# Attention in front of two mixture layers: memory product as two column halves, deeper buffers, a new table of task priorities

## The chip, the cores and the metric

The kernel runs on one core of a Trainium2 chip, in one launch. The metric is the device time of that launch in microseconds (us), the median of several runs; less is better.

## What is computed

Three stages in float32 (B, H, S, D = 4, 8, 576, 64; 2304 tokens, width 512):

```python
scores = where(causal, -1e9, scale * q @ k.T)          # per batch and head
local  = softmax(scores) @ v
q_p    = where(q > 0, q, exp(q) - 1) + 1                # the features
mem    = (q_p @ M_prev) / (q_p @ z_prev + 1e-6)
x      = g * mem + (1 - g) * local                      # g = sigmoid(beta), one per head
x      = (silu(x @ w_gate) * (x @ w_val)) @ w_out       # first layer, d_ff 1536
out    = quadratic_gate(x @ w_in) @ w_out2              # second layer, d_ff 2048
```

## The kernel before, in words

**Two plans.** The program is recorded as tasks. A task has an engine, an estimated duration, a priority number, the tasks that it needs and the buffer places that it holds. `Plan.order` (line 179 on) walks through an estimated time and on each engine starts the ready task of the lowest number, provided that free places are there; the order so found is emitted, and each engine then runs its own list strictly in that order. There are two plans. The first holds the attention and the part of the first layer that can be done early; the second holds the rest of the two layers. The second plan's lists are the same in both kernels.

**The first plan.** The attention is cut into 16 pairs (4 batches x 4 pairs of heads), `Attention.pair`, line 400 on. For a pair:

- SP loads K, Q, V, z and M (`load`, `load_v`, `load_z`, `load_M`).
- PE transposes K and Q into `K`, `S` (`tk`, `tm`, `tq`, lines 497 to 509).
- Features: ACT `min` and `exp`, VectorE (DVE) `phi`, then GpSimd (POOL) `w` and two `fold` (lines 540 to 551, tile `e`), DVE `nrm`, POOL `pn` (line 561, tile `p`); PE transposes `p` (`tp`, lines 567 and 570) into `P`.
- Scores: PE multiplies query chunk c (0 to 3) with the c+1 key chunks that the mask leaves, both heads side by side in the row halves of the array (`qk`, line 611; tiles `s0c` and `s1c` for the two heads), and the last 64 queries of both heads in one full product (`qk4`, line 642, tiles `s40`, `s41`). DVE adds the mask and takes the minimum (`mx`, line 622), ACT takes the exponential and its sum (`ex`, line 629) into the probability tiles `a0` to `a3`, and `a4`.
- DVE adds up and inverts the sums of a head, POOL scales each probability tile (`.sc`, line 697, nine per pair), PE transposes it (`t4`, `t03`, `t02`, `t01`, `t13`, `t12`, `t11`; lines 708, 710, 731, 748), ACT or DVE copies it to the tiles `R0`, `R1` (`.cp`, line 436; the table `COPY` names the engine).
- Output: `av1` (256 columns) and `av0` (320 columns) add the memory product (line 775, one product on the whole array: `MZ` is block diagonal over the two heads) and the products of V with the transposed probabilities, the two heads side by side in the column halves of the array (line 782). ACT and DVE split the result into `x`, and SP stores it to `xs` in DRAM (`x_out`, line 805).

The same plan decodes 12 weight units of the first layer: ACT and DVE steps, then three POOL instructions (lines 875, 878, 911). `EARLY` holds the priorities of the 12. As soon as 512 tokens of `xs` are there, `load_x` fetches them as four tiles `xh` (there are four places, so a group of tokens waits for the one before), and `early_unit` multiplies them (line 1031; 12 matmuls per unit, in two tasks of six, 36 units in all). ACT copies the result to `gvo`, and it is stored. These 432 matmuls depend on nothing of the pair at work, so they are PE's filler. `GROUP_AT` and `X_AT` are their priorities.

**What sets the order.** A task's number is 100 times the number of its pair plus the entry of its name in the table `ORDER`. The entries before reach from about -2300 to 2700, so the name counts for as much as several pairs.

**Places.** `AB` is the number of places for each of the tiles `a0` to `a3`, of which a pair needs two. `RB1` and `RB0` are the places per head for `R1` and `R0`. The tiles `e`, `p` and `x` have one place each (`plan.cap`, line 340 on).

Of the kernel before, what the change touches and what calls it, by code (L numbers as in the profile page):

```python
# [10 lines left out]
F32R = mybir.dt.float32r  # L11
# [7 lines left out]
P = 128  # L19
B, H, S, D = 4, 8, 576, 64  # L20
# [8 lines left out]
D1 = 8  # L29
UNITS1 = 12  # L30
BANKS = 5
AB, RB1, RB0 = 2, 1, 1
NOACT = 4
AHEAD = 30
CUTS = (0, 2, 4)
EARLY = (-695.6332, 2783.9892, 1285.5157, 4826.1976, -587.204, 1099.0329, 1783.7958, 812.7126, 3810.6396, 6743.5654, -296.1106, 490.4918)
XH, GVO = 4, 3
OWN = 2
XB, OP, RAW, HP, TP, WA = 12, 5, 3, 3, 3, 5
# [1 line left out]
UNITS, HALVES = 20, 5  # L41
PHASES = (2, 3, 3)

GROUP_AT, X_AT = (38662.3623, 35325.2542, 46229.556), (412.8002, 381.1663, 182.3662)

FIRST = (0, 8, 1, 2, 9, 3, 4, 10, 5, 6, 11, 7)
BLOCK = 512
# [13 lines left out]


ORDER = {
    "load": -940.6324,
    "load_v": 203.5903,
    "load_z": -887.0432,
    "load_M": -747.8821,
    "tk": -333.4689,
    "tm": -812.4048,
    "tq": 461.8326,  # L70
    "tk.cp": -890.2619,
    "tm.cp": 1721.9097,
    "tq.cp": 1307.1915,
    "min": 1423.9267,
    "exp": 311.185,
    "phi": 204.0583,
    "w": -1122.4349,
    "fold": -293.9033,
    "nrm": -731.8656,
    "pn": 1733.8628,  # L80
    "tp": 580.7614,
    "tp.cp": -62.0868,
    "tp4.cp": -2.2349,
    "qk": -1311.8398,
    "mx0": -1620.4126,
    "ex0": -960.1039,
    "mx1": -339.7968,
    "ex1": 2676.0763,
    "qk4": 521.5218,
    "mx4": -2277.3531,  # L90
    "ex4": 135.8776,
    "sum0": -780.2454,
    "sum1": -1647.8821,
    "t4.sc": 1505.0802,
    "t4": 592.7662,
    "t4.cp": 1106.002,
    "t03.sc": 264.3754,
    "t03": -818.1143,
    "t03.cp": -181.4909,
    "t02.sc": 771.2966,  # L100
    "t02": 487.7659,
    "t02.cp": -616.6291,
    "t01.sc": 772.9989,
    "t01": -20.2777,
    "t01.cp": -716.0608,
    "t13.sc": 304.2471,
    "t13": -447.9362,
    "t13.cp": -1725.7614,
    "t12.sc": 567.7268,
    "t12": -326.082,  # L110
    "t12.cp": 134.7649,
    "t11.sc": -27.9381,
    "t11": 430.1817,
    "t11.cp": -973.0528,
    "av0": 39.9166,
    "av0.hi": -241.9974,
    "av0.lo": 159.5083,
    "av1": -394.4432,
    "av1.hi": -361.6833,
    "av1.lo": -1110.4372,  # L120
    "x_out": 105.4227,
}
COPY = {"tk": "ACT", "tm": "ACT", "tq": "DVE", "tp": "ACT", "tp4": "ACT", "t4": "ACT", "t03": "ACT", "t02": "ACT", "t01": "DVE", "t13": "ACT", "t12": "DVE", "t11": "DVE"}


def f32(ap):
# [3 lines left out]
class Inst:  # L130


    def __init__(self, tag):
        self.tag, self.left, self.held, self.slot = tag, 0, False, None


class Plan:
# [4 lines left out]
    LAT = {"PE": 220, "ACT": 165, "DVE": 150, "POOL": 120, "SP": 650, "DMA": 950}  # L142
    RELEASE = 90

    def __init__(self, start=None, over=0):

        self.over = over
        self.tasks, self.caps, self.taken, self.start = [], {}, {}, start or {}
# [10 lines left out]
    def add(self, eng, dur, prio, fn, deps=(), uses=(), lat=0, behind=None, port=False):  # L159


        t = {"eng": eng, "port": port, "dur": dur + (0 if eng in ("SP", "DMA") else self.over), "prio": (prio, len(self.tasks)), "fn": fn, "uses": list(dict.fromkeys(uses)),
             "lat": lat + self.LAT[eng], "next": [], "follow": [], "wait": 0, "n": len(self.tasks)}
        for d in deps:
            d["next"].append(t)
            t["wait"] += 1
        for x in ([] if behind is None else behind if isinstance(behind, list) else [behind]):
            x["follow"].append(t)
            t["wait"] += 1
        for u in t["uses"]:  # L170
            u.left += 1
        self.tasks.append(t)
        return t
# [99 lines left out]
def c_fp(*cols):  # L273
    return sum(4 * n / 2.4 + 5 for n in cols) + 30


def c_two(*cols):


    return sum(4 * n / 2.4 + 5 for n in cols) + 2 * max(cols) / 2.4 + 30  # L280


def c_tr(n):
# [40 lines left out]
class Attention:  # L324
# [3 lines left out]
    def __init__(self, ctx, tc, plan, q, k, v, M_prev, z_prev, beta, cst, xs):  # L328
        self.tc, self.nc, self.plan = tc, tc.nc, plan
        nc = tc.nc  # L330
# [1 line left out]
        self.ident = cst["ident"]  # L332
        self.xs = xs
        pool = lambda name, bufs: ctx.enter_context(tc.tile_pool(name=name, bufs=bufs))
        self.ld, self.bt, self.ph = pool("ld", 2), pool("bt", 2), pool("ph", 1)
        self.st, self.ap, self.at = pool("st", 2), pool("ap", AB), pool("at", 1)
        self.sm, self.ac = pool("sm", 3), pool("ac", 1)
        self.ps = ctx.enter_context(tc.tile_pool(name="aps", bufs=1, space=PSUM))
        for tags, n in ((("kn", "qn", "vn", "zb", "a4", "K", "S", "P", "QZ", "MZ"), 2),
                        (("a0", "a1", "a2", "a3"), AB), (("R1_0", "R1_1"), RB1),  # L340
                        (("R0_0", "R0_1"), RB0), (("e", "p", "x"), 1), (("mn",), 3), (("bank",), BANKS)):
            for t in tags:
                plan.cap(t, n)

# [55 lines left out]
    def pair(self, b, n):  # L400
# [6 lines left out]
        nc, pl = self.nc, self.plan  # L407
# [7 lines left out]
        def add(eng, dur, name, fn, deps=(), uses=(), port=False):  # L415
            t = pl.add(eng, dur, num * 100 + ORDER[name], fn, deps, uses, port=port)
            t["name"] = name
            return t
# [179 lines left out]
        def scores(c):  # L598
# [6 lines left out]

            def qk():
                out = [psum(f"s{h}{c}", places[h]) for h in range(2)]
                step = kl // 2 if kl > 256 else kl
                for k0 in range(0, kl, step):
                    for h in range(2):  # L610
                        nc.tensor.matmul(out[h][:, k0:k0 + step], st["S"][halves[h], c * P:(c + 1) * P],  # L611
                                         st["K"][halves[h], k0:k0 + step], start=True, stop=True,
                                         tile_position=(h * 64, 0), skip_group_check=True)

            t_q = add("PE", c_two(kl), "qk", qk, [t_k, t_S], [*places, i_K, i_S, i_a[0, c], i_a[1, c]])
            for h in range(2):
# [138 lines left out]

        def mk_x():
            if "x" not in st:
                st["x"] = self.at.tile([P, 2, S], F32R, name="x", tag="x")
            return st["x"]

        def av(rg, deps):
# [10 lines left out]

            def f():
                o = psum(name, i_o)
                nc.tensor.matmul(o[:, 0:w], MZ().rearrange("p h d -> p (h d)"), st["P"][:, q0:q0 + w],  # L775
                                 start=True, stop=False, skip_group_check=True)
                for i, (c0, c1, kc, at_) in enumerate(terms):
                    n_ = c1 - c0
                    for h in range(2):
                        R = mk_R(rg, h)  # L780
                        r = R[:, at_:at_ + n_] if rg else R[:, at_[0], at_[1]:at_[1] + n_]
                        nc.tensor.matmul(o[halves[h], c0:c1], st["vn"][:, kc, h], r, start=False,  # L782
                                         stop=i == len(terms) - 1, tile_position=(0, h * 64), skip_group_check=True)
# [4 lines left out]
            def lo():  # L788
                nc.vector.tensor_sub(mk_x()[:, 1, q0:q0 + w], st[name][:, 0:w], f32(mk_x()[:, 0, q0:q0 + w]))

            cols = [c1 - c0 for c0, c1, *_ in terms]
            t = add("PE", c_fp(w) + c_two(*cols), name, f, deps + t_P + [l_v, t_M],
                    [i_o, i_P, i_v, i_M, *(i_R1, i_R0)[rg]])
            t = add("ACT", c_act(w), name + ".hi", hi, [t], [i_o, i_x])
            return add("DVE", c_dve2(w), name + ".lo", lo, [t], [i_o, i_x])
# [240 lines left out]
def tile_attention_two_moe(  # L1036
# [76 lines left out]


    with ExitStack() as actx:
        plan = Plan(over=50)
        wts.pooled = True
        wts.begin(actx, plan, {"raw": 2, "wA": 3, "wS": 1}, "a", "pool")
        plan.cap("w1", UNITS1)
# [463 lines left out]
```

## Time and profile before

| | |
|---|---|
| median of 3 runs | 1101.46 us (1099.88 to 1101.58) |
| profiled execution, own time | 1103.3 us |
| its span, first to last instruction | 1101.5 us |
| mean granted TensorE clock | 0.985 of full speed |
| PE busy over the span | 1058.4 us (96%) |
| POOL busy over the span | 212.9 us (19%), all of it in the first plan |

The profile shows one execution. A busy share over the whole span is an average of stages with different limits, so the stretch of the first plan has to be looked at by itself: its last attention product starts at 303.86 us, and its last filler ends where the second plan's matmuls run on without a break, at 363.80 us.

### The profile page before, as it was taken

What the parts mean: (1) busy time and instruction counts of PE and PEld (TensorE: products, weight loads), DVE (VectorE), ACT (ScalarE), POOL (GpSimd) and SP (SyncE); (2) the same over time, 40 slices, a digit from 0 to 9 for tenths busy, and PEclk for the clock granted to TensorE, in tenths of its full rate; (3) what the DMA queues carried; (4) which work ended last, traced back from release to release, by engine and by line L of the source; (5) the groups of instructions that cost most, each with busy time, mean ns of one, the idle gap of its engine ahead of it and who ended that gap; (6) DMA issues with size and microseconds to landing.
All of it is one profiled execution on the core that took longest, in us unless ns stands there. A gap on an engine that the chain in (4) does not pass through costs nothing.

```text
span 1101.5 us, 17845 instructions
## 1 busy us (share of the span) xinstructions
PE 1058.4 (96%) x6160; PEld 883.5 (80%) x6160; DVE 666.0 (60%) x1514; ACT 579.6 (53%) x1330; POOL 212.9 (19%) x285
## 2 busy tenths in 40 slices
PE   5779999999989999999999999999999999999998
PEld 3546677777778988888988888888899999899997
DVE  5767755655400687886867866673656668543443
ACT  6668777777511244543544434464555555444443
POOL 5888976654500000000000000000000000000000
PEclk9689999999999999999999999999999999999999
DMA  5464644444282888983995869999898887955422
GB/s 138 126 180 129 182 119 114 129 124 143 88 272 90 278 309 300 331 292 98 370 339 187 317 246 346 371 361 412 341 376 295 328 317 286 405 192 194 173 77 77
DMA packets 175722, 260.19 MB, mean 236 GB/s; under 512 B 71952, under 2 KB 100624, under 8 KB 175632
## 3 DMA queue, kind: packets, MB, share of 16 engines
q1 hardware_dynamic: 175056, 258.00, 67.3%
q8 instruction: 49, 0.80, 0.3%
q10 hardware_dynamic: 576, 1.05, 0.2%
q14 instruction: 41, 0.34, 0.1%
HBM read 177.21 MB, written 81.79 MB: 235 GB/s over the span
## 4 chain that ended last, share of the span: by engine, by line
PE 77%; DMA 2%; POOL 1%; DVE 1%; ACT 1%; issue 1%; DVEq 0%; ACTq 0%; POOLq 0%
PE mm L1031 25%; PE acc L1523 18%; PE mm L1272 16%; PE acc L1367 13%; PE av L782 2%; PE s L611 1%; POOL a L697 1%; DMA xs<-x 1%; PE av L775 1%; PE t L731 1%; DMA xh<-xs 1%; PE t L748 0%; PE s L642 0%; ACT t L1256 0%; ACT a L629 0%
## 5 line engine op out<-in xcount | busy, mean ns | idle before, releaser
L1523 PE MATMUL acc<-wu,h 128*128 128x512 f32 x864 | 211.1, 392 | 5.0 <-DVE h L1189 4.0
L1031 PE MATMUL mm<-xb,wu 128*128 128x512 f32 (+1 forms) x1008 | 202.4, 360 | 0.0
L1031 PEld LDWEIGHTS mm<-xb,wu 128*128 128x128 f32 x1008 | 171.1, 190 | 28.4
L1523 PEld LDWEIGHTS acc<-wu,h 128*128 128x128 f32 x864 | 157.4, 189 | 35.1 <-DVE h L1189 2.3
L1272 PE MATMUL mm<-xb,wu 128*128 128x256 f32 x1296 | 168.4, 283 | 0.6 <-ACT mm L1343 0.6
L1272 PEld LDWEIGHTS mm<-xb,wu 128*128 128x128 f32 x1296 | 164.1, 192 | 4.8 <-ACT mm L1343 1.0
L1367 PE MATMUL acc<-h,wu 128*128 128x512 f32 (+1 forms) x720 | 151.7, 368 | 0.0
L1367 PEld LDWEIGHTS acc<-h,wu 128*128 128x128 f32 x720 | 125.6, 189 | 22.3
L1186 ACT CAST h<-t 128x512 fp32r<-128x512 f32 (+1 forms) x140 | 80.5, 577 | 80.4 <-DVE t L1262 31.2
L1256 ACT ACTIVATE t<-mm,half 128x512 f32<-128x512 f32 (+1 forms) x80 | 51.6, 645 | 120.8 <-PE mm L1272 74.0
L1031 PE MATMUL mm<-xh,wu 128*128 128x512 f32 x432 | 111.6, 407 | 2.8 <-DMA xh<-xs 2.8
L1189 DVE TENSOR_TENSOR h<-t,h 128x512 fp32r<-128x512 f32 (+1 forms) x140 | 88.1, 635 | 41.4 <-ACT h L1186 40.6
L697 POOL TENSOR_SCALAR a<-a,r,OGP 128x512 f32<-128x512 f32 (+3 forms) x144 | 97.4, 686 | 30.0 <-PE tk L497 14.3
L1031 PEld LDWEIGHTS mm<-xh,wu 128*128 128x128 f32 x432 | 79.7, 190 | 20.4 <-issue 3.6
L1262 DVE SCALAR_TENSOR_TENSOR t<-mm,t 128x512 f32<-128x512 f32 (+1 forms) x80 | 50.9, 636 | 73.9 <-ACT t L1259 73.9
L1079 ACT COPY gvo<-mm 128x512 f32<-128x512 f32 (+1 forms) x80 | 42.7, 542 | 79.6 <-PE mm L1031 74.7
L629 ACT ACTIVATE a<-a,mn 128x512 f32<-128x512 f32 (+3 forms) x128 | 70.9, 556 | 18.4 <-DVE mn L622 17.7
L622 DVE CUSTOM_DVE_ANT_0 a<-s,mask 128x512 f32<-128x512 f32 (+3 forms) x128 | 56.9, 485 | 21.1 <-PE s L611 18.1
L848 ACT ACTIVATE wA<-raw 128x512 f32<-128x512 f32 x64 | 42.6, 670 | 45.7 <-DMA raw<-in_moe_w_in_dram 15.2
L611 PE MATMUL s<-K,S 64*128 64x256 f32 (+2 forms) x384 | 52.0, 392 | 2.3 <-DVE mn L622 2.3
L782 PEld LDWEIGHTS av<-R,vn 128*64 128x64 f32 x448 | 30.2, 139 | 28.5 <-issue 10.3
L782 PE MATMUL av<-R,vn 128*64 128x320 f32 (+4 forms) x448 | 52.0, 371 | 0.1
(123 smaller groups left out, 1375.2 us busy)
## 6 DMA issues: line engine op xcount, KB each, us to landing
xb<-ys SPq DMA_DIRECT2D x93, 512.0 KB, 7.5
park<-wu SPq DMA_DIRECT2D x40, 512.0 KB, 7.4
wu<-park SPq DMA_DIRECT2D x40, 512.0 KB, 9.0
xb<-xs SPq DMA_DIRECT2D x32, 512.0 KB, 7.5
gv<-gv SPq DMA_DIRECT2D x32, 512.0 KB, 7.3
ys<-yo SPq DMA_DIRECT2D x31, 512.0 KB, 6.7
gv<-gvo SPq DMA_DIRECT2D x60, 256.0 KB, 2.3
raw<-in_moe_w_out_dram SPq DMA_DIRECT2D x28, 512.0 KB, 6.4
```

Of the source, the lines that this page charges most:

```text
L611: nc.tensor.matmul(out[h][:, k0:k0 + step], st["S"][halves[h], c * P:(c + 1) * P], st["K"][halves[h], k0:k0 + step], start=True, stop=True ...
L622: nc.vector.tensor_tensor_reduce(a, st[f"s{h}{c}"][:, 0:kl], self.mask0[:, 512 - kl:512], -0.125, 3.0e38, ALU.add, ALU.min, mn[:, o:o + 1])
L629: nc.scalar.activation(a, a, AF.Exp, bias=mn[:, o:o + 1], scale=-1.0, accum_out=sm[:, o, 0:1])
L697: nc.gpsimd.tensor_scalar(a, a, st["mn"]["r"][:, o:o + 1], self.OGP[:, n, o:o + 1], op0=ALU.mult, op1=ALU.mult)
L782: nc.tensor.matmul(o[halves[h], c0:c1], st["vn"][:, kc, h], r, start=False, stop=i == len(terms) - 1, tile_position=(0, h * 64), skip_grou ...
L1031: nc.tensor.matmul(out, kt_of(unit, pw, kt), x[kt][:, px, cols], start=(kt == 0 and i == 0), stop=(kt == KT - 1 and i == 2))
L1186: nc.scalar.copy(s["h"][:, 0], s["t"])
L1189: nc.vector.tensor_sub(s["h"][:, 1], s["t"], f32(s["h"][:, 0]))
L1256: nc.scalar.activation(mk_t(o), src(), AF.Relu, bias=half, scale=0.5)
L1272: nc.tensor.matmul(out, pair["k"](k, pw, j), y["x"][piece][:, px, j], start=first and not (i or j), stop=last and j == 1 and i == 2, skip_ ...
L1367: nc.tensor.matmul(state[m][:, 0:n], l, r, start=(begin and i == 0), stop=(end and i == 2), skip_group_check=True)
L1523: nc.tensor.matmul(state[m], s["h"][:, px, m * P:(m + 1) * P], unit["w"][:, pw], start=(begin and i == 0), stop=(end and i == 2), skip_gro ...
```

## The change

1. Places: `a0` to `a3` from 2 to 3, `R1` and `R0` from 1 to 2 per head, `e`, `p` and `x` from 1 to 2.
2. The memory product (line 775) is two products of 64 columns each, side by side in the column halves of the array, as the products of V behind it are.
3. The scores of 512 and 384 keys are one product per head instead of two of half the columns.
4. All numbers of `ORDER`, `EARLY`, `GROUP_AT` and `X_AT` are new. The entries of `ORDER` now reach from -39700 to 65700, while a pair still adds 100: the name of a task nearly always decides, not its pair.
5. `COPY`: `tq` and `t11` move from DVE to ACT, `t02` and `t13` from ACT to DVE.
6. The planner's estimates (`over`, `c_two`) are other numbers; they act on nothing but the order.

```diff
-AB, RB1, RB0 = 2, 1, 1
+AB, RB1, RB0 = 3, 2, 2
-GROUP_AT, X_AT = (38662.3623, 35325.2542, 46229.556), (412.8002, 381.1663, 182.3662)
+GROUP_AT, X_AT = (40287.3734, 1227.9649, 39653.4433), (22172.7616, -5282.0496, -22244.0768)
...
-    "load_v": 203.5903,
...
+    "load": -1120.8527, "load_v": 32212.637, "load_z": -1110.1537, "load_M": -1074.952, "tk": 24105.5411,
...
-    return sum(4 * n / 2.4 + 5 for n in cols) + 2 * max(cols) / 2.4 + 30
+    return sum(4 * n / 2.4 + 5 for n in cols) + 150
...
-        self.ld, self.bt, self.ph = pool("ld", 2), pool("bt", 2), pool("ph", 1)
+        self.ld, self.bt, self.ph = pool("ld", 2), pool("bt", 2), pool("ph", 2)
...
-                        (("R0_0", "R0_1"), RB0), (("e", "p", "x"), 1), (("mn",), 3), (("bank",), BANKS)):
+                        (("R0_0", "R0_1"), RB0), (("e", "p", "x"), 2), (("mn",), 3), (("bank",), BANKS)):
...
-                step = kl // 2 if kl > 256 else kl
-                for k0 in range(0, kl, step):
-                    for h in range(2):
-                        nc.tensor.matmul(out[h][:, k0:k0 + step], st["S"][halves[h], c * P:(c + 1) * P],
-                                         st["K"][halves[h], k0:k0 + step], start=True, stop=True,
-                                         tile_position=(h * 64, 0), skip_group_check=True)
+                for h in range(2):
+                    nc.tensor.matmul(out[h][:, 0:kl], st["S"][halves[h], c * P:(c + 1) * P], st["K"][halves[h], 0:kl],
+                                     start=True, stop=True, tile_position=(h * 64, 0), skip_group_check=True)
...
-                nc.tensor.matmul(o[:, 0:w], MZ().rearrange("p h d -> p (h d)"), st["P"][:, q0:q0 + w],
-                                 start=True, stop=False, skip_group_check=True)
+                for h in range(2):
+                    nc.tensor.matmul(o[halves[h], 0:w], MZ()[:, h], st["P"][:, q0:q0 + w], start=True, stop=False,
+                                     tile_position=(0, h * 64), skip_group_check=True)
```

**How the order moves, first place: POOL, from the first scaled probability tile on.** Lines 697 and 649 are the scaling, 540/544/551 and 495/499/506 the features, 875/878/911 and 828/831/864 the weight decode, 516 the task `pn`. Before:

```order
L697 TENSOR_SCALAR a3_319<-a3_319,r_305,OGP_190 128x512
L551 TENSOR_TENSOR e_364<-e_364 128x9x32
L697 TENSOR_SCALAR a2_333<-a2_333,r_305,OGP_190 128x384
L551 TENSOR_TENSOR e_364<-e_364 128x9x16
L697 TENSOR_SCALAR a1_379<-a1_379,r_305,OGP_190 128x256
L697 TENSOR_SCALAR a0_395<-a0_395,r_305,OGP_190 128x128
L875 TENSOR_TENSOR wS_483<-wL_488,wS_483 128x512
L697 TENSOR_SCALAR a3_325<-a3_325,r_305,OGP_190 128x512
L878 TENSOR_TENSOR wA_440<-wA_440,wS_483 128x512
L697 TENSOR_SCALAR a2_346<-a2_346,r_305,OGP_190 128x384
L911 TENSOR_TENSOR wu_532<-wA_440,wu_532 128x512
```

And with the change, where the pair's last tile is row 51:

```order
L649 TENSOR_SCALAR a3_325<-a3_325,r_320,OGP_190 128x512
L495 TENSOR_TENSOR e_353<-p_420,zb_312 128x512
L499 TENSOR_TENSOR e_353<-p_420,zh_314 128x64
L649 TENSOR_SCALAR a2_351<-a2_351,r_320,OGP_190 128x384
L506 TENSOR_TENSOR e_353<-e_353 128x9x32
L649 TENSOR_SCALAR a1_371<-a1_371,r_320,OGP_190 128x256
L506 TENSOR_TENSOR e_353<-e_353 128x9x16
L495 TENSOR_TENSOR e_439<-p_475,zb_384 128x512
L499 TENSOR_TENSOR e_439<-p_475,zh_386 128x64
L649 TENSOR_SCALAR a0_382<-a0_382,r_320,OGP_190 128x128
```

Before, the second weight step stands between the scales of the first pair, and five units are decoded ahead of the last scale of the third pair. With the change one unit stands at the very start, two more lie ahead of that scale, and the features of the second and third pair (`e_353`, `e_439`) lie between the scales of the first.

**Second place: PE, at the first transposes of probabilities** (731, 748, 683 and 700 are transposes, 611 and 564 the scores). Before, the first pair's transposes stand together and then the second pair's scores of 512 keys, in steps of 256:

```order
L509 MATMUL tq_427<-ident_60,qn_348 128x128 x4
L731 MATMUL t03_453<-ident_60,a3_319 128x128 x4
L731 MATMUL t02_477<-ident_60,a2_333 128x128 x3
L748 MATMUL t11_499<-ident_60,a0_395 128x128
L748 MATMUL t11_499<-ident_60,a1_379 128x128 x2
L731 MATMUL t13_517<-ident_60,a3_325 128x128 x4
L611 MATMUL s03_525<-K_339,S_359 128x256
```

With the change a transpose of the first pair is followed by the second pair's scores of the same chunk, undivided:

```order
L683 MATMUL t03_455<-ident_60,a3_325 128x128 x4
L564 MATMUL s03_468<-K_333,S_413 128x512
L564 MATMUL s13_469<-K_333,S_413 128x512
L683 MATMUL t02_485<-ident_60,a2_351 128x128 x3
L564 MATMUL s02_494<-K_333,S_413 128x384
L564 MATMUL s12_495<-K_333,S_413 128x384
L700 MATMUL t01_529<-ident_60,a0_382 128x128
L700 MATMUL t01_529<-ident_60,a1_371 128x128 x2
```

**Third place: PE, late in the attention, with the change.** The last four filler rows (line 984) of a block of 126 matmuls of the second token group, and what follows; `s03_3635` and `s40_3644` belong to the pair before the last:

```order
L984 MATMUL mm_3580<-xh_3311,wu_838 128x512 x3
L984 MATMUL mm_3580<-xh_3323,wu_838 128x512 x3
L984 MATMUL mm_3590<-xh_3311,wu_1189 128x512 x3
L984 MATMUL mm_3590<-xh_3323,wu_1189 128x512 x3
L683 MATMUL t03_3616<-ident_60,a3_3224 128x128 x4
L660 MATMUL t4_3625<-ident_60,a4_0_218 128x128 x4
L662 MATMUL t5_3630<-ident_60,a4_0_218 128x128
L564 MATMUL s03_3635<-K_3157,S_3182 128x512
L564 MATMUL s13_3636<-K_3157,S_3182 128x512
L594 MATMUL s40_3644<-K_3157,QZ_0_226 128x288
```

Before, no more than 12 filler matmuls stand together ahead of the last attention product, and 210 of the 432 are ahead of it; with the change 330 are ahead of it and 102 behind.

## Rows read from the trace of the kernel before

**Rows 1.** The page: busy time of the engines; PE and its granted clock in 40 slices.

```profile
PE 1058.4 (96%) x6160; PEld 883.5 (80%) x6160; DVE 666.0 (60%) x1514; ACT 579.6 (53%) x1330; POOL 212.9 (19%) x285
...
PE   5779999999989999999999999999999999999998
...
PEclk9689999999999999999999999999999999999999
```

**Rows 2.** Busy time by stretch: stretch, length, busy us (instructions) of PE, PEld, DVE, ACT, POOL, then granted clock.

```profile
0.00:20.00 20.00, 12.79 (x63) 8.99 (x63) 10.78 (x51) 10.93 (x30) 7.82 (x30) 1.00 0.53 125
20.00:40.00 20.00, 11.62 (x47) 7.02 (x47) 13.71 (x29) 12.01 (x33) 15.94 (x18) 0.68 0.64 166
40.00:60.00 20.00, 15.72 (x89) 11.32 (x89) 15.39 (x43) 14.11 (x40) 19.02 (x20) 0.76 0.44 117
60.00:80.00 20.00, 14.09 (x89) 9.22 (x91) 12.94 (x34) 13.74 (x39) 16.10 (x19) 0.84 0.60 164
80.00:306.00 226.00, 221.51 (x1529) 162.11 (x1529) 131.88 (x456) 162.99 (x495) 154.03 (x201) 1.00 0.46 132
306.00:364.00 58.00, 55.24 (x243) 45.13 (x238) 1.77 (x4) 10.99 (x20) 0.00 (x0) 0.97 0.52 176
```

**Rows 3.** What PE waited for in 0 to 80 us: total us, times, longest.

```profile
PE t L731 <- POOL a L697: 7.5, 4, 3.3
PE t L748 <- POOL a L697: 6.9, 3, 3.9
```

**Rows 4.** POOL's groups in 5 to 310 us: shape, count, busy us, mean ns of one, idle before.

```profile
L697 POOL TENSOR_SCALAR a<-a,r,OGP 128x512 f32<-128x512 f32 (+3 forms) x144 | 97.4, 686 | 30.0 <-PE tk L497 14.3 <-PE tp L570 7.1 <-DVE r L688 4.2
L551 POOL TENSOR_TENSOR e<-e 128x288 f32<-128x288 f32 (+1 forms) x32 | 22.0, 687 | 0.4
L540 POOL TENSOR_TENSOR e<-p,zb 128x512 f32<-128x512 f32 x16 | 20.6, 1289 | 31.6 <-ACT P L436 9.9 <-DVE r L688 9.0 <-DVE p L535 5.5
L561 POOL TENSOR_TENSOR p<-p,nrm 128x576 f32<-128x576 f32 x16 | 18.9, 1179 | 9.9 <-DVE nrm L557 6.4 <-PE s L611 1.9 <-DVE mn L622 1.6
L911 POOL TENSOR_TENSOR wu<-wA,wu 128x512 fp32r<-128x512 f32 x12 | 16.5, 1377 | 3.7 <-ACT wu L909 2.5 <-DVE mn L622 1.1
L875 POOL TENSOR_TENSOR wS<-wL,wS 128x512 f32<-128x512 f32 x12 | 16.2, 1349 | 9.1 <-ACT wL L872 9.0
L878 POOL TENSOR_TENSOR wA<-wA,wS 128x512 f32<-128x512 f32 x12 | 15.9, 1328 | 0.3
L544 POOL TENSOR_TENSOR e<-p,zh 128x64 f32<-128x64 f32 x16 | 5.3, 331 | 0.0
```

**Rows 5.** POOL in order of time: start us, us, tile [idle before], first and third pair's scales.

```profile
21.79 0.77 POOL L697 TENSOR_SCALAR a<-a,r,OGP 128x512 f32<-128x512 f32 x1
...
81.47 0.82 POOL L697 TENSOR_SCALAR a<-a,r,OGP 128x576 f32<-128x576 f32 x1
```

**Rows 6.** PE in order of time, the end of the attention.

```profile
285.49 0.92 PE L611 MATMUL s<-K,S 64*128 64x256 f32 x8
286.35 1.67 PE L1031 MATMUL mm<-xh,wu 128*128 128x512 f32 x6
287.85 0.60 PE L567 MATMUL tp<-ident,p 128*128 128x128 f32 x4
...
289.80 0.60 PE L775 MATMUL av<-P,MZ 128*128 128x256 f32 x2
290.33 0.87 PE L782 MATMUL av<-R,vn 128*64 128x256 f32 x8
291.13 0.81 PE L775 MATMUL av<-P,MZ 128*128 128x320 f32 x2
291.87 2.27 PE L782 MATMUL av<-R,vn 128*64 128x320 f32 x20
...
306.07 18.40 PE L1031 MATMUL mm<-xh,wu 128*128 128x512 f32 x78
...
327.81 1.62 PE L1031 MATMUL mm<-xh,wu 128*128 128x512 f32 x3 [2.76 <-DMA xh<-xs]
```

More of the change, by code (lines that the diff above doesn't have):

```diff
@@ L35 @@
 CUTS = (0, 2, 4)
-EARLY = (-695.6332, 2783.9892, 1285.5157, 4826.1976, -587.204, 1099.0329, 1783.7958, 812.7126, 3810.6396, 6743.5654, -296.1106, 490.4918)
+EARLY = (-227.011, 30507.2865, 11290.2095, 7544.105, -18399.491, 13953.3813, 24196.0052, 17946.6642, 10825.913, 34187.5841, 1817.5643, 4835.322)
 XH, GVO = 4, 3
@@ L63 @@
 ORDER = {
-    "load": -940.6324,
-    "load_v": 203.5903,
[L66 to L121, printed above, removed]
-}
-COPY = {"tk": "ACT", "tm": "ACT", "tq": "DVE", "tp": "ACT", "tp4": "ACT", "t4": "ACT", "t03": "ACT", "t02": "ACT", "t01": "DVE", "t13": "ACT", "t12": "DVE", "t11": "DVE"}
+    "load": -1120.8527, "load_v": 32212.637, "load_z": -1110.1537, "load_M": -1074.952, "tk": 24105.5411,
+    "tm": -22020.4108, "tq": 2281.8105, "tk.cp": -17020.8154, "tm.cp": -10058.7697, "tq.cp": 6308.8913, "min":
+    -7579.4036, "exp": 1208.5469, "phi": -8414.6604, "w": -4059.7015, "fold": -13963.2611, "nrm": 2167.0733,
[8 rows of a table added]
+    "x_out": -26201.0151,
+}
+COPY = {"tk": "ACT", "tm": "ACT", "tq": "ACT", "tp": "ACT", "tp4": "ACT", "t4": "ACT", "t03": "ACT", "t02": "DVE",
+        "t01": "DVE", "t13": "DVE", "t12": "DVE", "t11": "ACT"}
 def f32(ap):
@@ L143, with __init__ @@
     RELEASE = 90
-    def __init__(self, start=None, over=0):
+    def __init__(self, start=None, over=None):
         self.over = over
@@ L159, in add @@
     def add(self, eng, dur, prio, fn, deps=(), uses=(), lat=0, behind=None, port=False):
-        t = {"eng": eng, "port": port, "dur": dur + (0 if eng in ("SP", "DMA") else self.over), "prio": (prio, len(self.tasks)), "fn": fn, "uses": list(dict.fromkeys(uses)),
+        t = {"eng": eng, "port": port, "dur": dur + (self.over.get(eng, 0) if self.over else 0), "prio": (prio, len(self.tasks)), "fn": fn, "uses": list(dict.fromkeys(uses)),
              "lat": lat + self.LAT[eng], "next": [], "follow": [], "wait": 0, "n": len(self.tasks)}
@@ L757, in mk_x @@
             if "x" not in st:
-                st["x"] = self.at.tile([P, 2, S], F32R, name="x", tag="x")
+                st["x"] = self.at.tile([P, 2, S], F32R, name="x", tag=f"x{i_x.slot}")
             return st["x"]
@@ L791, in av @@
             cols = [c1 - c0 for c0, c1, *_ in terms]
-            t = add("PE", c_fp(w) + c_two(*cols), name, f, deps + t_P + [l_v, t_M],
+            t = add("PE", c_two(w, *cols), name, f, deps + t_P + [l_v, t_M],
                     [i_o, i_P, i_v, i_M, *(i_R1, i_R0)[rg]])
@@ L1115, in tile_attention_two_moe @@
     with ExitStack() as actx:
-        plan = Plan(over=50)
+        plan = Plan(over={"PE": 15, "ACT": 40, "DVE": 40, "POOL": 50})
         wts.pooled = True
```

8 rows, old and new, of the table ORDER are left out of this document.

## The prediction

> **What bounds the kernel now.** The page comes first: PE is busy 96% of the span, so only time in which PE stands still, runs slow, or works longer than it must can be won [rows 1]. The 40 slices show where that is: the first three slices have PE at 5, 7 and 7 tenths, with a granted clock below full in the same place, and nearly all later ones have nines [rows 1]. So the next view is the table of stretches. In the first 80 us PE is busy 54.2 us, and since the granted clock is 0.68, 0.76 and 0.84 in three of the four stretches (means of its two levels, 1.2 and 2.4 GHz, behind PE's waits), that is worth 12.79 + 11.62 x 0.68 + 15.72 x 0.76 + 14.09 x 0.84 = 44.5 us at full speed [rows 2]. So 35.5 us are lost there. From 80 to 306 us, the rest of the attention, PE stands still 4.5 us in 226, and behind it 2.8 us in one wait for a transfer [rows 2, 6]. The list of waits says for whom PE stood in the first 80 us: 14.4 us are transposes that wait for POOL's scaled probabilities [rows 3]. POOL is busy up to 19.02 of 20 us there, and has 0 to do after the attention [rows 2].
>
> From the same rows: a filler matmul takes 18.40 / 78 = 0.236 us [rows 6], and a pair takes PE (221.51 - 210 x 0.236) / 14 = 12.3 us, since 210 fillers and 14 of the 16 pairs fall into 80 to 306 us [rows 2]. On POOL a pair costs 97.4 / 16 = 6.1 us of scaling, (22.0 + 20.6 + 5.3) / 16 = 3.0 us of features and 1.2 us of `pn`, 10.3 us in all, and a weight unit 1.377 + 1.349 + 1.328 = 4.05 us [rows 4]. So POOL is the slower of the two only as long as it decodes about a unit per pair (14.3 against 12.3) and PE has no filler. That is the state of the first 80 us.
>
> **The start.** The landmark is the last scaling of the third pair, since behind it PE has three pairs' work. Before, POOL needs from 21.79 to 82.29 us for it, 60.5 us from the first scaling [rows 5]. Its list between the two holds 18.3 us of scaling, 7.4 of features, 2.4 of `pn` and five and a third units, 21.6: 49.6 us, so POOL waited 10.9 us. With the change the same stretch of POOL's list holds the same 18.3 us of scaling, 9.0 of features (two pairs ahead instead of one), 1.2 of `pn` and two units, 8.1: 36.6 us. Without any wait the landmark comes at 21.8 + 36.6 = 58.4 us, 23.9 us earlier; with all 10.9 us of waiting left, at 69.3, 13 us earlier. The waits should get fewer: they come from the single places (the second pair's scores have no `a` tiles until the first pair's are transposed, the next features no `e` and `p`), and these are what is added; PE's list now has each transpose followed by the scores that take its place. Against it: the first unit now stands ahead of all features on POOL, and its load ahead of the first K on SP. POOL is idle 12 us of its first 20 [rows 2], which covers 4.05 us, but the features themselves may come up to 4 us late; I take 2. PE's own work at full speed between the same two points is about 44.5 - 12.8 + 2.3 = 34 us before [rows 2, 5] and much the same tasks after, in 36.6 us; so what slow clock is left costs directly. I take **-17 us**, ends -24 and -10. The units that were moved back are decoded with the fourth to twelfth pair, one per pair: 14.3 us of POOL beside 12.3 + 3.9 us of PE (162 fillers in that part, 0.236 each, over 10 pairs), so the cover is there, but thin: without the fillers POOL would cost PE 2 us a pair.
>
> **The products.** The memory product does the same columns in the same time, two halves side by side as the V products are. What can be won is the change between array modes. A run of six fillers behind scores takes 1.50 us instead of 6 x 0.236 = 1.42, and the memory product of 320 columns between column halves takes 0.74 us where 320/256 of the 0.53 us of the other would be 0.66 [rows 6]. So each side of a mode change costs about 0.08 to 0.1 us, and a change about 0.18. Counted in PE's list up to the last attention product there are 139 changes before (32 of them from the memory product into the V products) and 125 with the change: the 32 are gone, but 29 come in at the head of the product, because what stands ahead of it is now of another mode. 14 x 0.18 = 2.5; I take **-2 us**, ends -3 and 0. The Trainium skill, TensorEngine Tiling (Array Packing), section Tiling Modes, says that changing the tiling mode drains the engine. The rows agree with a price of 0.18 us; by that rule counted inside the product alone, 32 x 0.18 = 5.8 us would be won, and the sum below would be -22.
>
> The undivided scores do the same columns in 64 steps fewer; no row shows a price of a step between two equal ones, and six 512-column fillers in a row leave none to be seen, so 0, ends -1 and +1. The weight loads of the memory product double in number (64 columns each); PEld is busy 162 us of 226 and lies beside PE [rows 2], so 0. The copies that change engine: ACT is busy 163 and DVE 132 of 226 us, neither is the bound, and the two lists get about as much as they give: 0; without that cover a copy of about 0.6 us would stand ahead of a V product. `over` and `c_two` act on the order alone.
>
> **The middle.** 4.5 us of standing still remain between 80 and 306 us [rows 2]. More places for `R`, `e`, `p` and `x` speak for less, names that outweigh pairs for more: 0, ends -3 and +6.
>
> **The change of token groups.** The next four `xh` can be fetched only when the last filler has read the old ones. Before, that costs 2.76 us at 327.81 plus the slow clock behind it, (1 - 0.97) x 55.24 = 1.7: 4.4 us [rows 2, 6]. With the change this place is behind the block of 126, with two sixes of fillers (2.8 us), fourteen transposes and a pair's largest scores to cover it, about 6 us. I take **-2 us**, ends -4.4 and +3.
>
> **The tail.** The block keeps PE for 126 x 0.236 = 30 us while ACT, DVE and POOL run out of scores. Behind it lie some 3.3 pairs, 41 us of PE, with 42 fillers (10 us) between them, then 102 fillers, 24 us, that cover the last store and the second plan's first loads as 78 did before. The pairs interleave, and POOL has 16 us to do in 50; but each chain starts cold. I take **+3 us**, ends 0 and +9.
>
> **Sum:** -17 - 2 - 2 + 0 + 3 = -18. The profiled execution's own 1103.3 us become 1085.3; the median before is 1.84 us below that execution, so the forecast for the median is 1101.46 - 18 = **1083.5 us**. A difference under 0.2% (2.2 us) counts as none.
>
> **Rivals.**
> 1. *POOL's waits remain, and V is late* (0.18). The first V load has moved back on SP: it stands behind K and Q of the fifth pair, which wait for places, so the first `av1` may hold PE with everything behind it. Then the landmark comes with the old waits and some more, and PE gains 7 us instead of 17: 1094. For it: POOL waited on DVE and ACT too [rows 4], which get no places. Against it: PE has the second pair's scores and the fourth pair's K and Q transposes ahead of that `av1`.
> 2. *The tail starves, and the kernel is slower* (0.10). Behind the block PE goes back to the pace of the start: 60 us from 20 to 80 for three pairs, 20 each instead of 12.3 [rows 2]. For 3.3 pairs that is +25 us against -18: 1108. It decides where the tail loses more than 18 us net, 5.5 us a pair. For it: all fillers but 42 are spent before and after the pairs that need them. Against it: two and more pairs are under way at once there, with more places.
> 3. *Nothing comes of it* (0.06): the start is held by the chain from scores to scaling itself, not by places or units, the filler runs out elsewhere, and each gain returns as a wait: 1101.
>
> **Chances and range.** The forecast has 0.66 and lies between 1073 and 1091 by the ends of the start and the tail. With rival 1 the kernel is faster: 0.84. Rival 3 is mostly no difference, rival 2 slower: 0.05 and 0.11. The range goes from 1073, where start and tail both do their best, to 1100, which takes in rival 1 and leaves out rival 2 and most of rival 3.
>
> **What would show it.** Right: the last scaling of the third pair (line 649) ends between 58 and 69 us; the granted clock of 40 to 80 us is above 0.95; PE busy is over 17 us in the stretch from 40 to 60; the second plan's matmuls set in at about 346 us instead of 363.8, and all behind it lasts as long as before. Wrong: POOL still waits for 10 us before the landmark, waits of transposes for line 649 of more than 5 us behind the block of 126, or a first `av1` that waits for V.

## The result, and the profile after

The changed kernel takes **1073.7 us**, median of 4 runs (1072.09 to 1074.1), against 1100.88 us of the kernel before measured beside it: a ratio of 0.9751, 95% interval 0.9734 to 0.9768, or 27.2 us. The forecast was 1083.5 us, range 1073 to 1100: the sign and the range held, the gain came out half as large again. The profiled execution has a span of 1072.3 us and a time of 1074.1 (before 1101.5 and 1103.3).

First the page after, busy time and PE's slices, to be held against [rows 1].

```profile
PE 1043.9 (97%) x6096; PEld 865.0 (81%) x6096; DVE 666.1 (62%) x1514; ACT 577.8 (54%) x1330; POOL 214.2 (20%) x285
...
PE   6799999999999999999999999899999999999998
...
PEclk9899999999999999999999999999999999999999
```

Then the stretches, columns as in [rows 2]. The attention now ends near 307 us, so its last two stretches end earlier.

```profile
0.00:20.00 20.00, 10.70 (x40) 6.11 (x40) 10.45 (x47) 10.27 (x26) 10.65 (x33) 1.00 0.59 127
20.00:40.00 20.00, 13.79 (x71) 8.37 (x73) 11.06 (x40) 16.95 (x52) 16.63 (x21) 0.91 0.65 159
40.00:60.00 20.00, 19.34 (x132) 12.97 (x130) 15.16 (x52) 17.60 (x52) 17.10 (x20) 0.92 0.55 147
60.00:80.00 20.00, 18.54 (x141) 12.71 (x138) 17.27 (x57) 16.34 (x49) 18.56 (x24) 1.00 0.63 179
80.00:282.00 202.00, 201.30 (x1305) 144.16 (x1305) 122.28 (x387) 144.26 (x427) 142.87 (x177) 1.00 0.51 152
282.00:340.00 58.00, 58.00 (x358) 46.54 (x355) 19.64 (x54) 19.71 (x54) 8.36 (x14) 1.00 0.64 219
```

In the first 80 us PE's busy time at full speed is 10.70 + 13.79 x 0.91 + 19.34 x 0.92 + 18.54 = 59.6 us, against 44.5 before: 15.1 us. From 80 to 282 us PE stands still for 0.7 us, against 4.5 [rows 2], and behind that not at all. PE's waits in 0 to 80 us, against [rows 3]:

```profile
PE tk L452 <- DMA kn<-in_k_dram: 7.1, 1, 7.1
PE s L594 <- ACT R L391: 3.2, 1, 3.2
PE s L594 <- ACT QZ L391: 2.2, 2, 1.5
PE t L700 <- POOL a L649: 1.8, 3, 1.0
...
PE t L683 <- POOL a L649: 0.4, 1, 0.4
```

Of the 14.4 us of transposes that waited for POOL, 2.2 are left; PE starts later than before, at 7.1 us, since the first K now stands behind a unit's raw data. The landmark is the last scaling of the third pair, here the last of a row of five on POOL:

```profile
61.38 3.97 POOL L649 TENSOR_SCALAR a<-a,r,OGP 128x128 f32<-128x128 f32 x5
```

It ends at 65.35 us, against 82.29 [rows 5]. The end of the attention, in PE's order of time:

```profile
248.65 18.76 PE L984 MATMUL mm<-xh,wu 128*128 128x512 f32 x80
267.25 0.60 PE L683 MATMUL t<-ident,a 128*128 128x128 f32 x4
...
307.71 23.96 PE L984 MATMUL mm<-xh,wu 128*128 128x512 f32 x102
331.51 8.68 PE L984 MATMUL mm<-xb,wu 128*128 128x256 f32 x71
```

The first row is the end of the block of 126 fillers. Behind it, where the forecast feared cold chains, no row is marked with a wait longer than 0.3 us. The second plan's matmuls set in at 331.5 us instead of 363.8. Before, 13 of them (1.5 us) had been done early, so that is 30.8 us. From there on both kernels run the same lists; 1.6 us are given back, near 690 us, where the granted clock after is 0.96 for two stretches of 20 us and was 1.00 before, and 29.2 us remain at the end. The medians differ by 27.2; the profiled execution before took 2.4 us more than the median, the one after 0.4.

### The profile page after: what moved, and what is told of

It reads as the page before. It is cut to its first block, busy times and chain, and to the rows that moved or that the text cites. A ratio compares the mean times of both kernels' runs of the same rounds, so it can differ in the third digit from the quotient of the medians.

```text
span 1072.3 us, 17714 instructions
## 1 busy us (share of the span) xinstructions
PE 1043.9 (97%) x6096; PEld 865.0 (81%) x6096; DVE 666.1 (62%) x1514; ACT 577.8 (54%) x1330; POOL 214.2 (20%) x285
## 4 chain that ended last, share of the span: by engine, by line
PE 91%; ACT 3%; DVE 2%; DMA 2%; POOL 1%; issue 1%; SPq 0%; DVEq 0%; ACTq 0%
PE mm L984 27%; PE acc L1476 18%; PE mm L1225 16%; PE acc L1320 14%; PE av L735 4%; PE s L564 3%; PE t L683 2%; PE av L728 2%; PE s L594 2%; PE t L700 1%; DMA raw<-in_moe_w_gate_dram 1%; PE tk L452 1%; PE tp L522 1%; PE t L660 1%; ACT a L581 0%
## 5 line engine op out<-in xcount | busy, mean ns | idle before, releaser
L984 PE MATMUL mm<-xh,wu 128*128 128x512 f32 x432 | 108.9, 402 | 0.0
L649 POOL TENSOR_SCALAR a<-a,r,OGP 128x128 f32<-128x128 f32 (+3 forms) x144 | 100.5, 709 | 26.8 <-DVE r L640 19.1
L581 ACT ACTIVATE a<-a,mn 128x128 f32<-128x128 f32 (+3 forms) x128 | 71.2, 558 | 14.0 <-DVE mn L574 11.9
L806 DVE TENSOR_SCALAR wA<-wA 128x512 f32<-128x512 f32 x68 | 32.3, 477 | 35.3 <-ACT wA L801 35.0
L564 PE MATMUL s<-K,S 64*128 64x384 f32 (+3 forms) x256 | 49.8, 475 | 0.4 <-ACT R L391 0.2
L735 PEld LDWEIGHTS av<-R,vn 128*64 128x64 f32 x448 | 32.5, 139 | 21.8 <-issue 0.8
```

The costliest lines, as they stand in the source:

```text
L564: nc.tensor.matmul(out[h][:, 0:kl], st["S"][halves[h], c * P:(c + 1) * P], st["K"][halves[h], 0:kl], start=True, stop=True, tile_position= ...
L581: nc.scalar.activation(a, a, AF.Exp, bias=mn[:, o:o + 1], scale=-1.0, accum_out=sm[:, o, 0:1])
L649: nc.gpsimd.tensor_scalar(a, a, st["mn"]["r"][:, o:o + 1], self.OGP[:, n, o:o + 1], op0=ALU.mult, op1=ALU.mult)
L984: nc.tensor.matmul(out, kt_of(unit, pw, kt), x[kt][:, px, cols], start=(kt == 0 and i == 0), stop=(kt == KT - 1 and i == 2))
```

## The experiments

Two theories on the start stood against each other. **P**: the new places win it, since scores and features may run ahead. **L**: the new lists win it, with fewer units decoded early. Each run is compared with runs of the kernel before on the same chip.

**1. The old places under the new tables.**

```diff
-AB, RB1, RB0 = 3, 2, 2
+AB, RB1, RB0 = 2, 1, 1
```
and `ph`, `e`, `p`, `x` back to one.

> The changed kernel with the places of before: two `a` buffers per chunk, one `R`, `phi`, `e`, `p` and `x`; its tables, engines and column halves stay, and the planner orders anew. Theory P (the places win the start: the next scores and features can run while the last pair is still being transposed) expects most of the 17 us of the start to be lost again: 1086 us or more, PE waiting for POOL's scaled probabilities 8 us or more in the first 80 us, the last scaling of the third pair behind 75 us, and stalls back in 80 to 280 us. Theory L (the new order with fewer units decoded ahead wins it, and the places are seldom used) expects POOL's list, which holds 4 units ahead of that scaling against 3 after and 5 before, to decide: about 4 us, 1078, and that scaling at about 70 us.

1102.8 us, ratio 0.9993 (0.9978 to 1.0009): the whole gain is gone. The third pair's last scaling comes at 78.1 us, and PE's longest waits in the first 80 us are

```profile
PE t L700 <- POOL a L649: 10.6, 3, 6.4
...
PE t L683 <- POOL a L649: 6.1, 5, 2.1
```

So P's expectation is met: without the places the new tables are worth nothing.

**2. The new places under the old tables.** The reverse edit of the kernel before.

> The kernel before with the places of the change alone (three `a` buffers per chunk, two `R`, two `phi`, `e`, `p` and `x`); its tables, engines and undivided memory product stay, and the planner orders anew. Theory P expects a gain of 8 to 15 us over the kernel before, 1086 to 1093, since scores and features no longer wait for places. Theory L expects 0 to 4 us, 1097 to 1101: the old tables still put five units ahead of the third pair's last scaling, as before, and PE's wait for POOL in the first 80 us stays above 10 us.

1100.7 us, ratio 0.9976 (0.9961 to 0.999). L's expectation is met: 2.6 us, and transposes still wait 11.4 us for POOL in the first 80. The third pair's scaling comes at 75.5 us, yet the second's only at 73.5 (before 61.5): the planner, given places, mixed the pairs in another way, and in the first 80 us PE is busy 51.8 us, less than the 54.2 before. So run 1 speaks for P and run 2 for L: neither places nor tables win anything worth the name alone, and both theories are wrong as they were put.

**3. The new places, the order kept.** The kernel before with a spare place that the planner may hand out but may not count on, so that the lists of PE, ACT, DVE and POOL stay those of before.

```diff
-free = {tag: [i for i in range(n) if ...
+free = {tag: [i for i in range(n + MORE.get(tag, 0)) if ...
-if all(len(free[k]) >= v for ...
+if all(len(free[k]) - MORE.get(k, 0) >= v for ...
```

> The kernel before with one more place for each of `a0` to `a3`, `R`, `phi`, `e`, `p` and `x`, and the planner made to keep the order of before: the lists of PE, ACT, DVE and POOL are those of before, tile for tile. Theory P (a place is worth its wait) expects the 10.9 us that POOL waited in its first 82 us to shrink, and 4 to 11 us in all: 1090 to 1097. Theory F (a place is worth something only to a list that starts work in it early, since each engine takes its list in order) expects no difference, 1100 to 1102, and the last scaling of the third pair at 82 us as before.

1100.1 us, ratio 0.9983 (0.9967 to 0.9999); the scaling ends at 81.65 us. Theory F comes far nearer than P, though it expected nothing at all: a place alone is worth about 2 us. When the 432 fillers of the two traces are matched by their number, 0.6 us of it come before 130 us and 2.1 more between 151 and 253.

**4. The old start shifts, the new places.** The twelve numbers of EARLY as before; all else as in the change.

> The changed kernel with the old start shifts of the loads (the twelve numbers of before in EARLY), so that weight units and loads are taken up as early as before; places, names and the rest stay. Four units instead of three stand on POOL ahead of the third pair's last scaling, and none ahead of the first pair's. Theory L expects the start to be lost in large part: 8 to 16 us slower than the change, 1082 to 1090. Theory P expects one unit of 4 us more on POOL at most: 0 to 4 us, 1074 to 1078.

1101.5 us, ratio 0.9996 (0.9979 to 1.0012): all 27 us lost, more than L expected. The scaling ends at 89.2 us, and fillers now stand in PE's list ahead of their transfers:

```profile
PE mm L984 <- DMA xh<-xs: 7.9, 2, 5.9
PE t L700 <- POOL a L649: 6.1, 2, 5.8
```

**5. One start shift.** `EARLY[4]` from -18399.491 to -1050.0, so that K is loaded first and the planner orders anew.

> The changed kernel with one number of EARLY changed, so that the first K is loaded ahead of the first weight unit's raw data. In the change PE starts at 7.12 us, in the kernel before at 4.45. If the first 7 us are on the path, PE starts at about 4.5 us and up to 2.7 us are won: 1071. If POOL's chain sets the start whatever PE does in its first 7 us, the gain is under 0.7 us; and where the order that the planner makes from it puts one unit less ahead of the features, the last scaling of the third pair may still come later than the 65.35 us of the change (its row on POOL is 85 instead of 80): then it is up to 3 us slower.

1087.2 us, ratio 0.9852 (0.9823 to 0.9881): PE starts at 4.5 us, and some 11 us are lost by the ratios (0.9852 against 0.9751; the spans of the two profiled executions differ by 12.5), far outside what was expected. The scaling ends at 75.0 us. One number of a table that fits moves every list, and some four tenths of the gain with it.

**6. The same, the order kept.** Only K's three transfers are issued first.

```diff
+out.insert(sp[0], out.pop(k))
```

> The changed kernel with the first K's three transfers issued ahead of the first weight unit's raw data, all else in the order of the change. PE then starts at about 4.5 us instead of 7.12. If PE's first transposes and scores are on the path, 1 to 2.7 us are won: 1071 to 1073, a ratio of 0.973 to 0.974. If the features that stand behind the first unit's three steps on POOL hold the start, the unit comes about 1 us later by the move, and nothing is won or up to 1 us lost.

1072.9 us, ratio 0.973 (0.9706 to 0.9753), not to be told from the change. Matched by number, the first K transposes come 2.66 us earlier, those of the fourth pair, at 32 us, no earlier, and the end of the attention 0.43 us earlier. So of the 2.66 us no more than 0.43 was on the path.

**7 and 8. POOL's load in the kernel before.** My forecast had POOL as the engine that holds PE in the first 80 us. First, two of its three steps of the first five units are left out (the cut shows one of the two):

```diff
 def rest_b():
-    nc.gpsimd.tensor_mul(...)
+    if not s["off"]: nc.gpsimd.tensor_mul(...)
```

> The kernel before, order kept, without two of POOL's three steps of the first five weight units (the product of the two halves of a word and their sum, 10 instructions of 1.35 and 1.33 us, 13.4 us; these five units come out wrong). If POOL's list is what holds PE in the first 80 us, the last scaling of the third pair comes at 69 to 74 us instead of 82.3, PE's 14.4 us of waits for POOL shrink to under 6, and 8 to 13 us are won: 1088 to 1093. If POOL is held by ACT and DVE in its turn, the place of the removed work is taken by waits, and under 4 us are won.

1101.4 us, ratio 0.9987 (0.997 to 1.0004); the scaling ends at 81.26 us instead of 82.29. 13.4 us of POOL's work are gone and nothing is won by the medians. In place of the work stands a wait for the third step's input on ACT (POOL's longest in 0 to 82 us):

```profile
POOL wu L915 <- ACT wu L913: 14.9, 3, 6.7
```

So then all twelve units are taken off POOL: these two steps are left out, and the third is a fill that waits for nothing.

```diff
-lambda: two.tensor_sub(dst()[:, 1], src(), f32(dst()[:, 0]))
+lambda: nc.gpsimd.memset(f32(dst()[:, 1]), 0.0) if pooled else ...
```

> The kernel before, order kept, with all twelve weight units taken off POOL: two of its three steps are left out and the third is a fill that waits for nothing (the units come out wrong; ACT and DVE still do their part). With five units made lighter alone, POOL still stood up to 6.7 us in its list for the unit's copy on ACT. Theory U (the units in POOL's list hold the scaling, by their waits) expects the last scaling of the third pair at 62 to 72 us instead of 82, and 8 to 15 us won: 1087 to 1094. Theory R (each engine takes its list in order, the scaling waits for sums of scores that stand on PE behind the transposes of the pair before, and this round trip sets the pace) expects it within 4 us of 82 and under 4 us won: 1098 to 1102, with POOL idle most of the time. If units on POOL cause the lost time between 80 and 280 us, PE busy rises from 195.5 to 198 us or more there.

1097.3 us, ratio 0.9969 (0.9946 to 0.9992); the scaling ends at 79.93 us. The first pair's last scaling comes 9.7 us earlier than before (29.67 against 39.40), the second's 5.3 and the third's 2.4: what is won at first is lost again on the way. POOL in its order of time:

```profile
43.83 2.80 POOL L697 TENSOR_SCALAR a<-a,r,OGP 128x512 f32<-128x512 f32 x4 [12.58 <-PE tk L497]
...
70.20 1.26 POOL L540 TENSOR_TENSOR e<-p,zb 128x512 f32<-128x512 f32 x1 [11.87 <-ACT wA L848]
```

In brackets stands how long POOL was idle ahead of the row: 24 us in two holes, while PE still waits for `a`:

```profile
36.84 1.70 PE L611 MATMUL s<-K,S 64*128 64x256 f32 x4 [2.38 <-DVE mn L622]
...
54.15 0.55 PE L748 MATMUL t<-ident,a 128*128 128x128 f32 x3 [3.27 <-POOL a L697]
54.63 1.32 PE L611 MATMUL s<-K,S 64*128 64x256 f32 x8
```

The last two rows are the pattern: the next scores stand in PE's list behind transposes that wait for a scaling, and all that comes of those scores waits with them. So the decoding of units on POOL isn't the bound before: it filled time that POOL has left over. POOL's scalings are another matter; nothing was taken from them, and PE waits for them in this run too. What holds them up? ACT has the units' raw data in its list too, and waits there for the transfer. Its waits in 20 to 82 us, of this run and then of the kernel before:

```profile
ACT wA L848 <- DMA raw<-in_moe_w_gate_dram: 9.0, 4, 4.7
ACT wA L848 <- DMA raw<-in_moe_w_val_dram: 4.4, 2, 2.9
```

```profile
ACT wA L848 <- DMA raw<-in_moe_w_gate_dram: 5.8, 2, 4.4
...
ACT wA L848 <- DMA raw<-in_moe_w_val_dram: 1.8, 1, 1.8
```

With POOL relieved, ACT waits 13.4 us instead of 7.6 for raw data, and the exponentials stand behind that. After the change it waits 4.8. Traced back from the landmark by the releasers that the trace lets infer, the chain of before passes through two of these transfers, 9 us, and that of run 8 through three, 14 us. But a slow start doesn't need them: in run 1 (old places, new tables) ACT waits for no raw data from 20 to 82 us, its longest waits there being

```profile
ACT R L391 <- PE t L700: 7.5, 2, 3.7
ACT a L581 <- DVE mn L574: 7.0, 4, 3.5
```

and the landmark is late all the same. Whether the raw data or the round trip from scores to transposes holds the start of the old lists isn't told apart by my runs: to take the units off ACT as well wasn't tried.

**9. POOL's load in the changed kernel.** The third step of the first three units is done three times.

```diff
-lambda: two.tensor_sub(...)
+for _ in range(3 if self.seen <= 3 else 1): two.tensor_sub(...)
```

> The changed kernel, order kept, with POOL's last step of the first three weight units done three times instead of once: 6 instructions of about 1.38 us more, 8.3 us, all ahead of the last scaling of the third pair. If POOL's list sets PE's pace there, that scaling comes at about 73 us instead of 65.35 and the kernel takes 5 to 8 us more: 1079 to 1082. If POOL has slack there in the new order, under 2 us more. If PE starts to stand behind POOL for three pairs and its clock falls, 10 us or more.

1077.9 us, ratio 0.9773 (0.974 to 0.9805). The scaling ends at 70.62 us, 5.3 us later for 8.3 us of work. Matched by number, the fillers are 5.67 us late at 78 us and 5.09 us late from 204 us to the end of the attention. In the new lists POOL is for the larger part on the path, and a loss in the first 80 us is kept to the end of the attention: PE has next to no idle time behind it in which to make it up. Of the whole kernel the traces say 3.8 us by the spans and the ratios 2.4 (0.9773 against 0.9751, with intervals that overlap), so the runs alone don't show the loss clear of noise.

**10. No block.** `GROUP_AT[1]` set to `GROUP_AT[0]`.

> The changed kernel with the second of the three GROUP_AT shifts set to the first, so that the second group's fillers outrank nothing: the block of 126 fillers is gone, its fillers stand in sixes between the pairs' work and behind it; the pairs' own order on POOL is the same up to its 40th row and nearly so behind. The tail term of the forecast (a cold start behind the block costs 3 us, 0 to 9) expects a gain of 0 to 3 us over the change: 1071 to 1074. If the block instead saves something (each filler run of six between scores and V products costs mode changes, and one long run leaves the pairs' chains time to get ahead, so that PE finds all its operands ready behind it), the kernel is 2 to 8 us slower: 1076 to 1082, with PE busy less than 199 us in 80 to 280 us.

1072.4 us, ratio 0.9735 (0.971 to 0.9761), no difference from the change that can be told. PE is busy 199.62 of 200 us from 80 us on without the block, and 199.30 with it. Neither the cost that I put on it nor the saving that I then thought of is there.

**11 and 12. The products.** The memory product on the whole array, and the scores in two steps, each with all lists kept.

```diff
-for h in range(2):
-    nc.tensor.matmul(o[halves[h], 0:w], MZ()[:, h], ...)
+nc.tensor.matmul(o[:, 0:w], MZ().rearrange("p h d -> p (h d)"), ...)
```
```diff
-nc.tensor.matmul(out[h][:, 0:kl], ...)
+for k0 in range(0, kl, step): nc.tensor.matmul(out[h][:, k0:k0 + step], ...)
```

> The changed kernel, all lists kept, with the memory product on the whole array again. Counted in PE's list there are then 142 changes of mode instead of 125. At the forecast's 0.18 us per change that is 17 x 0.18 = 3.1 us slower, about 1077, a ratio of 0.978. Were only the change inside each product to count, it would be 32 x 0.18 = 5.8 us, 1079.5, a ratio of 0.980. If a change of mode is hidden by other waits in the new order, under 1 us.

> The changed kernel, all lists kept but that each pair of scores of 384 and 512 columns is again made in two steps, 64 matmul rows more. The forecast put nothing on this: 1073 to 1075, within 1 us of the change. If each of the two heads' matmuls, which stand side by side in the two row halves, costs something of its own at its start, 64 of some 0.06 us would be 4 us: 1077 to 1078.

1075.0 us, ratio 0.9751 (0.9731 to 0.9772), and 1074.6 us, 0.9748 (0.9725 to 0.9771): by the medians neither can be told from the change. The traces say more, since the lists are the same. A product of 320 columns with what stands around it, in the changed kernel and then in run 11 (start us, us):

```profile
279.53 1.77 PE L564 MATMUL s<-K,S 64*128 64x512 f32 x8
281.24 0.76 PE L728 MATMUL av<-P,MZ 128*64 128x320 f32 x4
281.82 2.23 PE L735 MATMUL av<-R,vn 128*64 128x320 f32 x20
283.98 0.92 PE L564 MATMUL s<-K,S 64*128 64x256 f32 x8
```

```profile
280.30 1.77 PE L564 MATMUL s<-K,S 64*128 64x512 f32 x8
282.00 0.81 PE L727 MATMUL av<-P,MZ 128*128 128x320 f32 x2
282.74 2.27 PE L734 MATMUL av<-R,vn 128*64 128x320 f32 x20
284.94 0.92 PE L564 MATMUL s<-K,S 64*128 64x256 f32 x8
```

Between the scores (row halves) and the V products (column halves) the changed kernel changes mode once, run 11 twice. From its start to the V products the memory product takes 0.74 us instead of 0.58, and the V products take 2.20 to the next row instead of 2.16. Product by product it is the same: one change more costs 0.20 us (0.15 at the product, 0.05 at the V products), two more about twice that, and where the number of changes is equal (a product behind transposes or fillers) the difference is 0.00. So 17 changes more are 3.4 us, near the 3.1 of the forecast's price. At the end of the attention less is to be seen: the fillers are 0.31 us early at 78 us, 0.85 us early at 93 us and 0.93 us late at the end. Four of the 17 changes lie ahead of 93 us, where PE waits anyway; of the 2.6 us of the 13 behind it, 1.8 remain, and most of the rest comes back at two places, near 149 and 164 us, where the changed kernel waits a few tenths of a us longer and run 11 doesn't. With the scores split the fillers are 0.25 us late at 78 us and 0.25 us at the end: the difference arises before 78 us, and the steps behind it cost nothing.

## Why the prediction was right, and where not

- **The start**, -17: by the stretches -15.1, and the landmark at 65.35 us lay in the 58 to 69 forecast. PE busy over 17 us in 40 to 60 came true with 19.34; the clock of 40 to 80 came to 0.92 and 1.00, a mean of 0.96. But the reason given was wrong for the kernel before. "POOL is the slower of the two" and its list of five units sets the landmark: runs 7 and 8 take these units away and the landmark moves by 1 and 2.4 us. I had read POOL's 10.9 us of waiting as what is left over, and its work as the bound; the units were filling time that the other engines' waits left free. For the changed kernel the sum by POOL's list does hold (36.6 us of work and 7.6 us of waits from the first scaling at 21.14 us, and run 9). So the landmark was hit with a right account of one kernel and a wrong one of the other, and that is luck in part. What the runs show of the cause: the places, the tables and EARLY win the start only together, since without one of them (runs 1, 2, 3 and 4) at most 2.6 us of 27 remain. That the next pair's scores ahead of the waiting transposes and the later loads are what does it is how I read the lists. It is argued and not shown: each of runs 1, 2 and 4 moves all the lists, and `COPY` and the planner's estimates were never changed by themselves.
- **The products**, -2: the price, 0.18 us a change, was right (0.20 by run 11), so 14 changes less are worth up to 2.8 us. What the forecast left out is that a price counts only where PE doesn't wait: of run 11's 3.4 us 0.9 to 1.2 arrived at the end of the attention. The Trainium skill (TensorEngine Tiling (Array Packing), Tiling Modes) says that a change of mode drains the engine. The 0.20 us of run 11 agree with that. Counted inside the product alone, 32 times, it does not come out: at 18 of the 32 products run 11 has no change more than the changed kernel, and there nothing is lost. **The scores**, 0: confirmed by run 12.
- **The middle**, 0 with ends -3 and +6: this step failed. PE's standing still fell from 4.5 to 0.7 us, 3.8 us, where I had left it. And some 6 us more are gone that stood in the profile as busy time: 30.8 - 15.1 (start) - 1.2 (product, as run 11 has it) - 4.4 (token groups) - 3.8 = 6.3. Of these, 1.0 is the slow clock of the start, which lasted until 82 us before (2.00 us of busy time from 80 to 82 at a granted clock of 0.51, against 1.00 after). Up to 1.6 may be the product, if its 14 changes show in full. The other 4 to 5 us have no place yet. The matmuls themselves have not become faster, though groups of fillers in 80 to 280 us look like it, before, after and in run 10:

```profile
L1031 PE MATMUL mm<-xh,wu 128*128 128x512 f32 x174 | 48.5, 414 | 0.0
```

```profile
L984 PE MATMUL mm<-xh,wu 128*128 128x512 f32 x288 | 73.9, 403 | 0.0
```

```profile
L984 PE MATMUL mm<-xh,wu 128*128 128x512 f32 x213 | 58.0, 409 | 0.0
```

That is 0.279, 0.257 and 0.272 us a filler, but run 10 is as fast as the change. A run of fillers counts the last one's whole length, 0.40 us, once, and the block makes of many runs one. From start to start a filler takes 0.232 us in both kernels (median), and a six takes 1.50 us with the change,

```profile
284.83 1.66 PE L984 MATMUL mm<-xh,wu 128*128 128x512 f32 x6
286.33 0.49 PE L700 MATMUL t<-ident,a 128*128 128x128 f32 x3
```

as it did before [rows 6]. Since a filler is shown 0.40 us long and the next starts 0.232 behind it, a wait of up to some 0.17 us between two of them would stand as busy time; that the missing 4 to 5 us are such short waits is an estimate that no run tests. Run 3 ascribes 2.1 us of this stretch to places alone, run 8 nothing of it to POOL's units (the fillers keep their 2.9 us from 130 to 319 us). Which part of the new order has the rest stays open.
- **The change of token groups**, -2: all 4.4 us of the profiled execution are won, the upper end. But the term moves from execution to execution: with the old lists there, this wait is 2.8 us before, 3.2 in run 3, and 0.7 and 0.8 at full clock in runs 7 and 8. So not all of it need belong to the change. **The tail**, +3: 0, with the block and (run 10) without it.
- **The sum**: -15.1 - 1.2 - 10.1 - 4.4 = -30.8 at the second plan, +1.6 given back later, where the forecast had -18; the 10.1 is the middle, 3.8 and 6.3. The second plan's matmuls, expected at about 346 us, set in at 331.5: this sign missed, and the range held by its lower end.
- **The rivals**: waits for V and a starving tail don't show. The third, that nothing comes of it, is the time that runs 1, 2 and 4 have, whatever their reasons.

## What to carry to other kernels

Where each engine takes a fixed list in order, places, order and start shifts are one thing: more places are worth little to a list that wasn't made for them (run 3), and a list fitted to them can lose much or all when one input moves (runs 1, 4 and 5). To find whether some work of a busy engine is the bound, take that work away with the lists kept: if the engine then idles and the end doesn't move, the work was only filling time. Compare runs with kept lists by matching instructions by number; that resolves tenths of a us where the medians resolve two. A group's busy time divided by its count isn't the price of one: ask when the next one starts.

## What the runs showed of the hardware that was not expected

- A change of the array's mode cost 0.20 us, the same at each product (run 11 against the change, row by row), while 17 of them moved the end of the attention by no more than 1.2 us: the rest fell into waits that PE had anyway.
- A matmul of 256 columns is no dearer as one of two than as half of a 512 one: 64 more steps, 0.0 us from 78 us to the end of the attention (run 12).
- PE's first 2.66 us, won by an earlier K, were gone at 32 us (run 6), while 8.3 us of work on POOL cost 5.1 us to the end of the attention (run 9).
